# Agent attention and MLP in one kernel: block maxima added by TensorE to four score chunks, new load order and banks at the head

## The chip, the cores and the metric

The kernel runs on one core of a Trainium2 chip. The metric is device time in microseconds (us), the median of several executions; lower is better.

## The reference, cut to what matters

```python
def _attn_ref(q, k, v, agents):            # q, k, v: 2 x 12480 x 128; agents: 2 x 49 x 128
    scale = 1.0 / np.sqrt(q.shape[-1])
    def sm(a, b):
        s = scale * (a @ b.transpose(0, 2, 1))
        s = s - s.max(-1, keepdims=True)
        e = np.exp(s)
        return e / (e.sum(-1, keepdims=True) + 1e-09)
    agent_v = sm(agents, k) @ v            # 49 x 128 for each of the two batches
    return (sm(q, agents) @ agent_v).astype(np.float32)

def _moe_ref(x, w_in, w_out):              # x: 24960 x 128, d_ff = 2048
    h = x @ w_in
    return (np.maximum(0.01 * h, h) @ w_out).astype(np.float32)
```

The output is `_moe_ref(_attn_ref(q, k, v, agents).reshape(24960, 128), w_in, w_out)`. w_in and w_out come as 64-bit floats; the kernel makes 32-bit floats of their two halves itself.

## The kernel before, in words

Since `sm(q, agents)` is a matrix P of 49 columns, `x @ w_in` is `P @ (agent_v @ w_in)`: the kernel computes M = agent_v @ w_in once for each batch and then multiplies P by M. Products of full precision are made of two fp32r parts ("hi" and "lo"). The leaky relu is 0.99 relu plus 0.01 of the linear part, which is P @ (M @ w_out), with `ww` = 0.01 w_in @ w_out and l = agent_v @ ww.

**Main loop.** 52 blocks of 480 rows, eight steps in each. A step is `mm1` (six products with M, L785), `relu` (ACT makes hi, L798; DVE makes lo, L799) and, two steps later, `mm2` (twelve products with w_out, L815) into one of two PSUM pairs, `turns`. `mm1` has two PSUM pairs of its own. The attention of q for later blocks, the whole of batch 1 and other side work are hung into the steps by `at(step, function)`.

**Head.** Before block 0 the kernel does batch 0's agent attention over K and V in 13 chunks each (c = 0 to 12, 960 rows in a chunk), the conversion of w_in and w_out in eight pieces (w0 to w7, w_in and w_out in turn; w7 in the loop), P of blocks 0 and 1, and M. For a chunk of K, TensorE makes scores in one PSUM bank (`k_score`, L380), DVE takes them into a running maximum (`k_run`, L391), ACT copies them to SBUF (`k_copy`, L394). After the last chunk `k_max0` to `k_max3` (L405 to L429) find the maximum of each agent and spread it over the partitions, `k_sub` subtracts it from each chunk on DVE (L347), `k_exp` is the exponential on ACT (L438), and `k_av32` the product with V (L504). For a piece of w: `conv_bits` (masks, DVE, L263 and L264), `conv_mant` and `conv_exp` (ACT), `conv_low`, `conv_sign`, `conv_mul` (DVE, L279, L286, L293); w_out pieces then `wo_hi_of` and `wo_lo_of`. `ww_tr`, `ww_copy` and `ww_mm` (L310, L317, L323) transpose w_in and add up w_in @ w_out. At the end `f_copy` (L513), `f_den` (L523), `f_tr` (L531), `f_rec` (L537), `f_avT` (L543), then `m_half` and `m_mm` (L565, L575) make M, which `m_hi_of` and `m_lo_of` (L596, L600) scale and split. `p_two` copies P of block 0 out of that of block 1 by three DMAs (L763).

**Order.** `Plan` is a list scheduler that runs while the kernel is built: each step of the head has an engine, an assumed cost and the steps it follows; what can begin first comes next, with a per-kind `slack` added to its key. The instructions of an engine run in that order. Where TensorE's plan has a gap, `heat` products (L963) fill it. Loads are issued on SP in the order of `ORDER` (k, q, w, v), nine chunks of k and v in flight. `users` is the order in which steps take turns in the bank that `aux()` gives (q products, transposes, maximum, denominator).

Of the kernel before, what the change touches and what calls it, by code (L numbers as in the profile page):

```python
# [18 lines left out]
class Plan:  # L19
# [16 lines left out]
    def emit(self, idle):  # L36
# [16 lines left out]
        while len(done) < len(self.steps):  # L53
# [11 lines left out]
            if eng == idle[0] and begin > self.free.get(eng, 0) + idle[2]:  # L65
                idle[1](int((begin - self.free[eng] - 50) / idle[2]))
# [6 lines left out]
def tile_agent_attention_then_leaky_mlp(  # L73
# [51 lines left out]
    NP = NF // 2  # L125
    LD = 9
# [3 lines left out]
    ORDER = "kqwwkkwkkwkkkwkkkkkqwvvvvwvvvvvvvvvwq"  # L130
# [44 lines left out]
    ones = const.tile([P, P], F32, name="ones")  # L175
# [208 lines left out]

    def k_run(b, c):
        ps = sc_t[b, c][:TP, :CH * NA]
        r = run.rearrange("p j a -> p (j a)")
        if c == 0:
            nc.vector.tensor_copy(r, ps)
        else:  # L390
            nc.vector.tensor_tensor(out=r, in0=ps, in1=r, op=ALU.max)  # L391
# [11 lines left out]
    def k_max0(u):  # L403
        rm = p1.tile([TP, NA], F32, tag="rm", name="rm")
        nc.vector.tensor_reduce(  # L405
            out=rm, in_=run.rearrange("p j a -> p a j"), axis=AX.X, op=ALU.max
        )
        mb[u] = rm

    def k_max1(u):  # L410
        ps = aux()
        nc.tensor.transpose(ps[:NA, :TP], mb[u], ident[:TP, :TP])
        mb[u] = ps

    def k_max1d(u):
        m = p1.tile([NA, 1], F32, tag="m", name="m")
        nc.vector.tensor_reduce(out=m, in_=mb[u][:NA, :TP], axis=AX.X, op=ALU.max)
        dg = p1.tile([NA, NA], F32, tag="rm", name="dg")
        nc.vector.tensor_scalar(dg, ident[:NA, :NA], m, None, ALU.mult)
        mb[u] = dg  # L420

    def k_max2(u):
        ps = aux()
        nc.tensor.matmul(ps[:TP, :NA], lhsT=ones[:NA, :TP], rhs=mb[u], start=True, stop=True)
# [38 lines left out]
    NH = NCH * CH // G  # L463

# [27 lines left out]
    def av_zero(b, first):  # L492

        if first:
            av_t[b] = avw[0][:, :C + 2]
        z = pre[:TP, 0, :C + 2]
        nc.tensor.matmul(av_t[b], lhsT=z[:, :P], rhs=z, start=first, stop=not first)

    def k_av32(b, h):

        c, g = divmod(h, CH // G)
        for j in range(g * G, (g + 1) * G):
# [3 lines left out]
                start=False, stop=False,  # L506
# [13 lines left out]
    def f_den(b):  # L520
# [26 lines left out]
    mp_t, wp_t, mp_pair = {}, {}, []  # L547
# [331 lines left out]
    at(6, wo_lo_of, w7)  # L879
    at(7, k_m, 0, NM, 1)  # L880
# [60 lines left out]
    with tc.manual_schedule():  # L941
# [4 lines left out]
        nc.vector.memset(ones, 1.0)  # L946
# [4 lines left out]
        for o, a, n in SLOTS:  # L951
# [3 lines left out]
            )  # L955
        nc.gpsimd.memset(pd, 0.0)
# [3 lines left out]
        def heat(n, start=False):  # L960
# [16 lines left out]
            "k": (lambda c: load_k(0, c), 1210), "v": (lambda c: load_v(0, c), 1280),  # L977
            "w": (load_w, 1250), "q": (load_q, 610),
        }
        ring, held = [], {"k": ("run", "copy"), "w": ("low", "sign"), "v": ("vdone",)}  # L980
        sent, come = [], []
        for what, c in loads:
# [12 lines left out]
            cost += {2: 1700, 7: 1200}.get(len(come), 0)  # L995
            add((what, c), "dma", cost, lambda: None, (), [("trip", what, c)] + come[-1:], lag=0)
            come.append((what, c))
        for c in range(NCH):
            for g in range(2):
                after = [("k", c)] + [(x, c - 4) for x in ("run", "copy") if c >= 4]  # L1000
                after += [("s", c, 0)] * g
                add(("s", c, g), "pe", 560, k_score, (0, c, g, True), after, lag=150)
            after = [("s", c, 1)] + [("run", c - 1)] * (c > 0)
            add(("run", c), "dve", 485, k_run, (0, c), after)
            add(("copy", c), "act", 400, k_copy, (0, c), [("run", c)])
# [27 lines left out]
        add("two", "sp", 1350, p_two, (1,), [last, ("send", "v", NCH - 1)], lag=2000)  # L1033
        for m in range(NM):
            add(("tr", m), "pe", 620, ww_tr, (m,), [("mul", 2 * m)], lag=250)
            add(("wcopy", m), "act", 500, ww_copy, (m,), [("tr", m)])
            if m < NM - 1:
                add(("wmm", m), "pe", 1170, ww_mm, (m,), [("wcopy", m), ("mul", 2 * m + 1), "avopen"] + [("wmm", m - 1)] * (m > 0))
        last = ("run", NCH - 1)
        for fn, eng, cost in (  # L1040
            (k_max0, "dve", 780), (k_max1, "pe", 300), (k_max1d, "dve", 480),
# [103 lines left out]
```

## Time and profile before

| | us |
|---|---|
| median of 3 runs (lowest, highest) | 961.69 (960.86, 963.61) |
| the profiled execution, its time | 962.66 |
| the profiled execution, its span | 960.6 |
| TensorE busy (share of the span) | 946.2 (98%) |
| DVE busy | 737.7 (77%) |
| ACT busy | 612.4 (64%) |
| GpSimd busy | 374.0 (39%) |

The span runs from the first to the last instruction of that execution; its time also has what lies around the span. Busy shares are averages over the head and the loop, which have different limits. The rows of the trace name engines PE (TensorE), PEld (its weight loads), DVE, ACT, POOL (GpSimd) and SP (the queue that issues loads); times in them are us from the span's start, and L504 is line 504 of the kernel before. Every fp32 product is two records.

### The profile page before, as it was taken

How to read it: one execution, taken by the hardware profiler on the slowest of the kernel's cores; microseconds unless marked ns; L12 is line 12 of the kernel's file. 1: busy time of each engine (PE TensorE's matmuls, PEld its weight loads, DVE VectorE, ACT ScalarE, POOL GpSimd, SP SyncE). 2: the span in 40 equal slices, each digit the busy share in tenths (PEclk: the TensorE clock that was granted, in tenths of full speed). 3: DMA queues.
4: the chain of work that ended last, by engine and by line, in shares of the span. 5: the costliest groups of instructions: out<-in, count | busy, mean ns of one | idle time of the engine just before them, and what ended most of it. 6: DMA issues, size and time to landing. Idle time of an engine off the chain costs nothing.

```text
span 960.6 us, 22990 instructions
## 1 busy us (share of the span) xinstructions
PE 946.2 (98%) x9478; PEld 879.6 (92%) x9478; DVE 737.7 (77%) x1067; ACT 612.4 (64%) x908; POOL 374.0 (39%) x546
## 2 busy tenths in 40 slices
PE   8899999999999999999999999999999999999998
PEld 7767888888899899999988899999999999999897
DVE  7767677777888888888877777777777777777774
ACT  6655566566676666666666666666666666666654
POOL 0002243234566566565444434333343333343420
PEclk9999999999999999999999999999999999999999
DMA  9930322312312323222121111211111111112110
GB/s 341 404 115 24 122 74 83 114 32 64 94 53 71 86 63 86 62 63 73 34 57 37 43 52 32 63 33 52 42 43 53 43 53 42 53 42 53 32 42 21
DMA packets 29043, 70.74 MB, mean 74 GB/s; under 512 B 4467, under 2 KB 17907, under 8 KB 28939
## 3 DMA queue, kind: packets, MB, share of 16 engines
q1 hardware_dynamic: 28795, 69.16, 23.5%
q8 instruction: 74, 1.21, 0.5%
q14 instruction: 30, 0.25, 0.1%
q10 hardware_dynamic: 144, 0.12, 0.0%
HBM read 43.22 MB, written 12.78 MB: 58 GB/s over the span
## 4 chain that ended last, share of the span: by engine, by line
PE 95%; DMA 2%; DVE 1%; ACT 1%; issue 1%; SPq 0%; ACTq 0%
PE turn L815 57%; PE h L785 28%; PE turn L650 2%; PE turn L826 2%; PE turn L380 1%; PE turn L472 1%; PE turn L504 1%; DMA kt<-in_k_dram 1%; DMA w<-in_w_in_dram 1%; PE sc L380 1%; DVE lo L799 0%; PE turn L963 0%; PE turn L323 0%; ACT hi L798 0%; PE turn L575 0%
## 5 line engine op out<-in xcount | busy, mean ns | idle before, releaser
L799 DVE SCALAR_TENSOR_TENSOR lo<-h,hi 128x960 fp32r<-128x960 f32 x416 | 479.0, 1151 | 191.6 <-ACT hi L798 191.5
L798 ACT ACTIVATE hi<-h 128x960 fp32r<-128x960 f32 x416 | 405.9, 976 | 293.7 <-PE h L785 277.5
L815 PE MATMUL turn<-hi,wo_hi 64*128 64x480 f32 x1664 | 420.2, 380 | 0.0
L815 PE MATMUL turn<-hi,wo_lo 64*128 64x480 f32 x1664 | 416.9, 376 | 0.0
L785 PE MATMUL h<-pT,m_hi 64*128 64x480 f32 x1664 | 338.6, 377 | 0.5 <-DVE lo L799 0.4
L815 PE MATMUL turn<-lo,wo_hi 64*128 64x480 f32 x1664 | 337.7, 375 | 0.0
L815 PEld LDWEIGHTS turn<-hi,wo_lo 64*128 64x128 f32 x1664 | 261.2, 184 | 10.0
L815 PEld LDWEIGHTS turn<-hi,wo_hi 64*128 64x128 f32 x1664 | 257.4, 184 | 11.4 <-issue 1.5
L785 PEld LDWEIGHTS h<-pT,m_hi 64*128 64x128 f32 x1664 | 236.0, 184 | 12.6 <-DVE lo L799 0.8
L815 PEld LDWEIGHTS turn<-lo,wo_hi 64*128 64x128 f32 x1664 | 237.1, 184 | 11.1
L785 PE MATMUL h<-pT,m_lo 64*128 64x480 f32 x832 | 242.7, 375 | 0.0
L785 PEld LDWEIGHTS h<-pT,m_lo 64*128 64x128 f32 x832 | 139.0, 184 | 5.7
L347 POOL TENSOR_TENSOR qlo<-qt,qhi 128x480 fp32r<-128x480 f32 x50 | 61.2, 1225 | 78.8 <-DMA kt<-in_k_dram 63.4
L347 POOL TENSOR_TENSOR pT<-pt,pT 64x480 fp32r<-64x480 f32 x50 | 61.0, 1220 | 60.4 <-ACT pT L750 60.4
L693 POOL COPY mx<-mx 32x15 f32<-32x15 f32 x50 | 9.4, 188 | 184.8 <-DVE mx L686 178.3
L347 POOL TENSOR_TENSOR d<-st,mm 64x375 f32<-64x375 f32 x50 | 41.3, 826 | 94.6 <-DVE mm L699 94.6
L849 POOL TENSOR_TENSOR oT<-oT 128x480 f32<-128x480 f32 x51 | 62.5, 1225 | 12.8 <-issue 10.0
L838 ACT COPY oT<-turn 128x480 f32<-128x480 f32 x102 | 52.0, 562 | 1.1 <-PE turn L815 1.1
L736 POOL TENSOR_TENSOR pd<-d,rs 64x375 f32<-64x375 f32 x50 | 40.9, 817 | 28.9 <-DVE rs L731 28.9
L650 PE MATMUL turn<-qhi,a_hl 64*128 64x240 f32 x208 | 47.3, 275 | 1.2 <-DVE m_lo L600 0.7
L693 POOL COPY sm<-sm 32x15 f32<-32x15 f32 x50 | 9.4, 188 | 98.1 <-DVE sm L716 98.1
L650 PE MATMUL turn<-qlo,a_hl 64*128 64x240 f32 x208 | 47.1, 272 | 0.0
(146 smaller groups left out, 905.4 us busy)
## 6 DMA issues: line engine op xcount, KB each, us to landing
kt<-in_k_dram SPq DMA_DIRECT2D x26, 480.0 KB, 6.4
qt<-in_q_dram SPq DMA_DIRECT2D x52, 240.0 KB, 2.9
pT<-pT SPq DMA_DIRECT2D x104, 120.0 KB, 2.3
out_dram<-oT SPq DMA_DIRECT2D x51, 240.0 KB, 2.0
vt<-in_v_dram SPq DMA_DIRECT2D x13, 520.0 KB, 9.5
vt<-in_v_dram SPq DMA_DIRECT2D x13, 487.5 KB, 4.5
w<-in_w_in_dram SPq DMA_DIRECT2D x4, 512.0 KB, 9.3
w<-in_w_out_dram SPq DMA_DIRECT2D x4, 512.0 KB, 8.9
```

What stands on the lines that cost most here:

```text
L347: eng.tensor_tensor(out=o, in0=x, in1=y, op=ALU.subtract)
L380: nc.tensor.matmul(ps[r, j * NA:(j + 1) * NA], lhsT=k_t[b, c][:, j, r], rhs=a_sb[:, b, :], start=True, stop=True,)
L650: nc.tensor.matmul(s_t[i][:, m, :h], lhsT=a_hl[i // BPB][r], rhs=x[r, m * h:(m + 1) * h], start=(s == 0 and n == 0), stop=(n == 1), skip_g ...
L693: by(i).tensor_copy(r[x, :, 1], r[y, :, 0])
L736: by(i).tensor_tensor(out=pd[:n, :, :A0], in0=d[:n], in1=w[:n].to_broadcast([n, NT, A0]), op=ALU.mult,)
L785: nc.tensor.matmul(ps[:, g, :NB], lhsT=w[b][r, cols(2 * p + g)], rhs=t[r, x], start=(n == 0), stop=(n == 2),)
L798: nc.scalar.activation(hi, ps, AF.Relu)
L799: nc.vector.scalar_tensor_tensor(out=lo, in0=ps, scalar=0.0, in1=hi.bitcast(F32), op0=ALU.max, op1=ALU.subtract,)
L815: nc.tensor.matmul(o[g][:, :NB], lhsT=w[r], rhs=x[r], start=start, stop=stop)
L826: nc.tensor.matmul(o[g][:, :NB], lhsT=w[b][r], rhs=t[r, x], start=False, stop=False)
L838: nc.scalar.copy(t[:, g], o[g][:, :NB])
L849: nc.gpsimd.tensor_tensor(out=t[:, 0], in0=t[:, 0], in1=t[:, 1], op=ALU.add)
```

## The change

Scores of chunks 9 to 12 of batch 0 stay in PSUM, in rows of 50 instead of 49 columns. After the maximum, `k_top` lets TensorE add minus the maximum to them, as one fp32r product of a matrix of ones with a matrix that has the maxima on its diagonal in two parts (`top`); `k_exp` reads them from PSUM. They have no `k_copy` and no `k_sub`. The products with V begin with these four chunks (`TURN`), and v is loaded in that order. Chunks 0 to 3 get their scores from products of full width (120 columns of weights), not two halves. `ORDER` is new. The closing zero product of the accumulation goes. The transpose and the two halves of M get PSUM banks of their own, and the transpose comes ahead of the denominator. Piece 1 of M, the third w_out product and `ww_part` move from the head into step 1 of the loop, the rest of M and of w7 to later steps. Heat is put in with 300 ns less in each gap, and none ahead of the last steps of the head. Costs and slacks of the plan are new.

```diff
-            if eng == idle[0] and begin > self.free.get(eng, 0) + idle[2]:
-                idle[1](int((begin - self.free[eng] - 50) / idle[2]))
+            gap = begin - self.free.get(eng, 0) - idle[3]
+            if eng == idle[0] and gap > idle[2] and name not in idle[4]:
+                idle[1](int(gap / idle[2]))
...
+    NS = 4
+    NW = 4
...
-    ORDER = "kqwwkkwkkwkkkwkkkkkqwvvvvwvvvvvvvvvwq"
+    ORDER = "qwkkwkwkkwkkqkkkkkkvvvvvwvvvvwwvvvvwq"
...
         ps = sc_t[b, c]
+        w = NA + late(b, c)
+        whole = b == 0 and c < NW
         for j in range(g * CH // parts, (g + 1) * CH // parts):
-            for r in (slice(0, HALF), slice(HALF, TP)):
+            for r in (slice(0, TP),) if whole else (slice(0, HALF), slice(HALF, TP)):
                 nc.tensor.matmul(
-                    ps[r, j * NA:(j + 1) * NA], lhsT=k_t[b, c][:, j, r], rhs=a_sb[:, b, :],
-                    start=True, stop=True,
+                    ps[r, j * w:j * w + NA], lhsT=k_t[b, c][:, j, r], rhs=a_sb[:, b, :],
+                    start=j == 0 or not late(b, c), stop=True,
+                    skip_group_check=late(b, c),
                 )
+    def late(b, c):
+        return b == 0 and c >= NCH - NS
...
     def k_max0(u):
...
+        for o in (0, HALF):
+            nc.vector.tensor_reduce(
+                out=wide[:, o:o + NA], in_=run.rearrange("p j a -> p a j"), axis=AX.X,
+                op=ALU.max,
+            ) if o == 0 else nc.vector.tensor_copy(wide[:, o:o + NA], wide[:, :NA])
...
     def k_max1d(u):
...
+        nc.vector.tensor_reduce(out=m, in_=mb[u][:EW, :TP], axis=AX.X, op=ALU.max)
+        nc.vector.tensor_scalar(top, less, m, None, ALU.mult)
+        r = slice(HALF, EW)
+        nc.vector.scalar_tensor_tensor(
+            out=top[r], in0=less[r], scalar=m[r], in1=top[r].bitcast(F32),
+            op0=ALU.mult, op1=ALU.subtract,
+        )
...
+    def k_top(b, c):
+
+        ps = sc_t[b, c][:TP, :CH * (NA + 1)].rearrange("p (j a) -> p j a", j=CH)
+        t = top[:, None, :].to_broadcast([EW, CH, NA + 1])
+        nc.tensor.matmul(ps, lhsT=ones, rhs=t, start=False, stop=True, skip_group_check=True)
...
+    TURN = [(n - NS) % NCH for n in range(NCH)]
...
     def f_tr(b):
         t = av_t[b]
+        if b == 0:
+            tr_t[b] = single("tr")
...
-        if h == 0:
-            mp_pair.append(single("mp"))
         c = slice(h * MC // 2, (h + 1) * MC // 2)
-        ps = mp_t[b, h / 2] = mp_pair[-1][:, c]
+        ps = mp_t[b, h / 2] = single("mp")[:, :MC // 2]
...
-    at(0, k_m, 0, 2)
-    at(0, conv_bits, w7)
-    at(1, conv_exp, w7, 0)
-    at(2, k_m, 0, 3)
+    at(1, k_m2, 0, 1)
+    at(1, ww_mm, NM - 2)
+    at(1, ww_part)
+    at(1, conv_bits, w7)
+    at(2, conv_exp, w7, 0)
     at(3, conv_exp, w7, 1)
     at(4, conv_mant, w7, nc.scalar)
     at(4, conv_sign, w7)
+    at(5, k_m, 0, 3)
     at(5, conv_low, w7)
-    at(5, conv_mul, w7, nc.vector)
-    at(6, ww_mm, NM - 1)
-    at(6, ww_end)
+    at(6, conv_mul, w7, nc.vector)
     at(6, wo_hi_of, w7, nc.scalar)
-    at(6, wo_lo_of, w7)
-    at(7, k_m, 0, NM, 1)
+    at(7, ww_mm, NM - 1)
+    at(7, ww_end)
+    at(7, wo_lo_of, w7)
+    at(8, k_m, 0, NM, 1)
...
-        add("two", "sp", 1350, p_two, (1,), [last, ("send", "v", NCH - 1)], lag=2000)
+        add("two", "sp", 1800, p_two, (1,), [last, ("send", "v", NCH - 1)], lag=2300)
...
-            (f_copy, "act", 230, "avend"), (f_den, "pe", 150, f_copy),
-            (f_tr, "pe", 250, f_den), (f_rec, "dve", 330, f_den), (f_avT, "act", 230, f_tr),
+            (f_copy, "act", 270, ("av", NH - 1)), (f_tr, "pe", 400, f_copy),
+            (f_den, "pe", 200, f_tr), (f_avT, "act", 270, f_tr), (f_rec, "dve", 330, f_den),
...
-        for n, fn, args in ((0, m_half, (0, 0)), (0.5, m_half, (0, 1)), (1, m_mm, (0, 1))):
+        for n in (0, 0.5):
...
+        add("go", "pe", 1300, lambda: None, (), [("mhi", 0), "two"])
...
-            (("tr", 1), ("wcopy", 1)), (k_max1, k_max1d), (k_max2, k_max3),
-            (("chain", 1, 2), ("chain", 1, 5)), (("tr", 2), ("wcopy", 2)),
-            (("tr", 3), ("wcopy", 3)), (f_den, f_avT),
+            (("tr", 1), ("wcopy", 1)), (("chain", 1, 2), ("chain", 1, 5)),
+            (k_max1, k_max1d), (k_max2, k_max3), (("tr", 2), ("wcopy", 2)),
+            (("tr", 3), ("wcopy", 3)), (f_den, f_rec),
...
-            plan.emit(("pe", heat, 270))
+            plan.emit(("pe", heat, 270, 300, (f_tr, f_den, ("mm", 0), ("mm", 0.5), "go")))
...
-        owner[0] = 0
-        ww_part()
```

## Rows read from the trace of the kernel before

**Rows 1.** Table of stages: us, engines' busy time (count), granted clock, DMA share, GB/s.
```profile
31.97:36.40 4.43, 4.43 (x41) 4.14 (x41) 2.73 (x7) 0.49 (x1) 0.00 (x0) 0.63 1.02 409
53.40:59.00 5.60, 4.79 (x29) 3.66 (x27) 2.85 (x8) 2.59 (x7) 0.00 (x0) 1.00 0.41 88
59.00:81.00 22.00, 19.12 (x144) 14.08 (x146) 15.82 (x22) 12.96 (x19) 1.58 (x3) 1.00 0.26 79
81.00:103.00 22.00, 22.00 (x251) 19.40 (x251) 15.14 (x23) 13.19 (x20) 7.51 (x13) 1.00 0.25 80
```

**Rows 2.** Chain of waits, head: start, length, engine, tile and line.
```profile
30.05 1.91 issue
31.97 0.84 PE sc L380 x21
...
38.63 4.59 PE turn L504 x80
...
53.43 0.43 PE turn L497 x2
...
54.26 0.49 PE turn L963 x2
...
56.88 0.86 PE turn L575 x2
...
58.92 1.04 PE h L785 x6
```

**Rows 3.** Timeline, block 0: start, length, engine, line, operation, [idle <-releaser].
```profile
64.15 0.49 PE L815 MATMUL turn<-hi,wo_hi 64*128 64x480 f32 x2
...
67.52 0.39 PE L650 MATMUL turn<-qlo,a_hl 64*128 64x240 f32 x2
...
75.76 1.13 PE L323 MATMUL turn<-w_out_sb,pre 128*128 128x128 f32 x8 [1.74 <-DVE w_out_sb L293]
...
80.83 0.60 PE L785 MATMUL h<-pT,m_hi 64*128 64x480 f32 x4
```

**Rows 4.** Timeline of SP: the issue of V's last chunk.
```profile
42.37 0.33 SPq L212 DMA_DIRECT2D vt<-in_v_dram  x1
```

**Rows 5.** DMA issues in 42.2 to 42.75: count, size, us to landing.
```profile
vt<-in_v_dram SPq DMA_DIRECT2D x1, 520.0 KB, 7.0
```

**Rows 6.** Timeline after the last score.
```profile
33.46 0.83 DVE L405 TENSOR_REDUCE rm<-run 120x49 f32<-120x392 f32 x1
...
35.15 0.41 PE L412 MATMUL turn<-ident,rm 120*49 120x120 f32 x1
...
35.90 0.24 DVE L419 TENSOR_SCALAR dg<-ident,m 49x49 f32<-49x49 f32 x1
```

**Rows 7.** Timeline of the tail: ACT and SP.
```profile
54.15 1.82 SPq L763 DMA_DIRECT2D pT<-pT  x3
...
55.43 0.27 ACT L543 COPY avT<-turn 128x128 f32<-128x128 f32 x1 [1.22 <-DVE den L537]
...
56.91 0.84 ACT L596 ACTIVATE m_hi<-mp,rec 128x256 fp32r<-128x256 f32 x2 [1.22 <-PE mp L565]
...
58.27 0.50 SPq L767 DMA_DIRECT2D pT<-pT  x1
```

**Rows 8.** Timeline of DVE: masks (L263) and last products (L293) of w chunks.
```profile
7.86 0.43 DVE L263 TENSOR_SCALAR em<-w 128x512 int32<-128x512 int32 x1 [0.41 <-DMA w<-in_w_in_dram]
...
12.65 0.68 DVE L293 TENSOR_TENSOR w_in_sb<-w_in_sb,e 128x512 f32<-128x512 f32 x1
...
36.06 0.41 DVE L263 TENSOR_SCALAR em<-w 128x512 int32<-128x512 int32 x1
...
40.45 0.43 DVE L263 TENSOR_SCALAR em<-w 128x512 int32<-128x512 int32 x1
...
48.87 0.69 DVE L293 TENSOR_TENSOR w_in_sb<-w_in_sb,e 128x512 f32<-128x512 f32 x1
...
55.51 0.67 DVE L293 TENSOR_TENSOR w_out_sb<-w_out_sb,e 128x512 f32<-128x512 f32 x1
```

More of the change, by code (lines that the diff above doesn't have):

```diff
@@ L174, in tile_agent_attention_then_leaky_mlp @@
     turn = const.tile([P, 2, 1], F32, name="turn")
-    ones = const.tile([P, P], F32, name="ones")
+    ones = const.tile([HALF + NA, TP], F32R, name="ones")
+    less = const.tile([HALF + NA, NA + 1], F32, name="less")
+    top = const.tile([HALF + NA, NA + 1], F32R, name="top")
+    wide = const.tile([TP, P], F32, name="wide")
     sel = const.tile([EW, P], F32, name="sel")
@@ L403, in k_max0 @@
     def k_max0(u):
[L404 to L408, printed above, removed]
+        for o in (0, HALF):
[3 more added lines that the diff above has]
+            ) if o == 0 else nc.vector.tensor_copy(wide[:, o:o + NA], wide[:, :NA])
     def k_max1(u):
         ps = aux()
-        nc.tensor.transpose(ps[:NA, :TP], mb[u], ident[:TP, :TP])
+        nc.tensor.transpose(ps[:EW, :TP], wide[:, :EW], ident[:TP, :TP])
         mb[u] = ps
     def k_max1d(u):
[L416 to L420, printed above, removed]
+        m = p1.tile([EW, 1], F32, tag="m", name="m")
+        nc.vector.tensor_reduce(out=m, in_=mb[u][:EW, :TP], axis=AX.X, op=ALU.max)
[5 more added lines that the diff above has]
+        )
     def k_max2(u):
         ps = aux()
-        nc.tensor.matmul(ps[:TP, :NA], lhsT=ones[:NA, :TP], rhs=mb[u], start=True, stop=True)
+        nc.tensor.matmul(ps[:TP, :NA + 1], lhsT=ones, rhs=top, start=True, stop=True)
         mb[u] = ps
@@ L490, in e_zero, with av_zero @@
         nc.gpsimd.memset(er[r].bitcast(F32), 0.0)
-    def av_zero(b, first):
-        if first:
-            av_t[b] = avw[0][:, :C + 2]
+    def av_zero(b):
+        av_t[b] = avw[0][:, :C + 2]
         z = pre[:TP, 0, :C + 2]
-        nc.tensor.matmul(av_t[b], lhsT=z[:, :P], rhs=z, start=first, stop=not first)
+        nc.tensor.matmul(av_t[b], lhsT=z[:, :P], rhs=z, start=True, stop=False)
     def k_av32(b, h):
-        c, g = divmod(h, CH // G)
+        n, g = divmod(h, CH // G)
+        c = TURN[n]
         for j in range(g * G, (g + 1) * G):
@@ L505, in k_av32 @@
                 av_t[b][o:o + NA], lhsT=s_sb[:, c, j, :], rhs=v_t[b, c][:TP, j, :],
-                start=False, stop=False,
+                start=False, stop=h == NH - 1 and j >= CH - 2,
             )
@@ L955, in tile_agent_attention_then_leaky_mlp @@
             )
+        nc.gpsimd.tensor_tensor(
+            out=less, in0=ident[:EW, :NA + 1], in1=ident[:EW, HALF:EW + 1], op=ALU.add
+        )
+        nc.gpsimd.tensor_scalar(less, less, -1.0, None, ALU.mult)
         nc.gpsimd.memset(pd, 0.0)
@@ L976, in tile_agent_attention_then_leaky_mlp @@
         fetch = {
-            "k": (lambda c: load_k(0, c), 1210), "v": (lambda c: load_v(0, c), 1280),
+            "k": (lambda c: load_k(0, c), 1210),
+            "v": (lambda n: load_v(0, TURN[n]), 1280),
             "w": (load_w, 1250), "q": (load_q, 610),
         }
-        ring, held = [], {"k": ("run", "copy"), "w": ("low", "sign"), "v": ("vdone",)}
+        ring, held = [], {"k": ("run",), "w": ("low", "sign"), "v": ("vdone",)}
         sent, come = [], []
@@ L994, in tile_agent_attention_then_leaky_mlp @@
             add(("trip", what, c), (what, c), 1500, lambda: None, (), sent)
-            cost += {2: 1700, 7: 1200}.get(len(come), 0)
+            cost += {2: 900, 6: 600, 8: 800, 15: 900}.get(len(come), 0)
             add((what, c), "dma", cost, lambda: None, (), [("trip", what, c)] + come[-1:], lag=0)
@@ L1001, in tile_agent_attention_then_leaky_mlp @@
                 after += [("s", c, 0)] * g
-                add(("s", c, g), "pe", 560, k_score, (0, c, g, True), after, lag=150)
+                add(("s", c, g), "pe", 560 if c >= NW else 860, k_score, (0, c, g, True), after, lag=150)
             after = [("s", c, 1)] + [("run", c - 1)] * (c > 0)
             add(("run", c), "dve", 485, k_run, (0, c), after)
-            add(("copy", c), "act", 400, k_copy, (0, c), [("run", c)])
+            if not late(0, c):
+                add(("copy", c), "act", 400, k_copy, (0, c), [("run", c)])
         for n in range(w7):
@@ L1077, in tile_agent_attention_then_leaky_mlp @@
         slack = {
[L1078 to L1080 removed]
+            "tr": 400, "wmm": 800, "wohi": 2000, "wolo": 1200, "bits": 400, "mant": 300,
+            "exp": 100, "low": 400, "sign": 800, "mul": 600, "sub": 600, "copy": 1200,
+            "run": 200, "wcopy": 200, "av": 200,
         }
```

62 lines of the change are left out of this document (34 added, 28 removed).

## The prediction

> **What bounds the kernel now.** I read the table of stages first. From 81 us on TensorE is busy without a gap (22.00 of 22.00), so every microsecond by which that state comes earlier is one of the total, and so is TensorE work that is taken out of what is left then; the diff takes none. Before it, in 59 to 81, TensorE is idle for 2.9 us, where block 0 starts up [rows 1]. So there are two questions: when does the first product of block 0 (L785) start, now 58.92, and how long is it from there to block 1's first, now 80.83, which is 21.9 us later [rows 2, 3].
>
> Second, the chain of waits. Before 58.92 it is TensorE from 38.6 on: the products with V (L504) run from 38.63 to 53.43 with little between them but transposes and heat, 0.92 us for a chunk of 16 records (4.59 for five). Then comes a serial tail: closing product, copy, heat, denominator, transpose, copy, two halves of M, a third piece of M, products of w_out [rows 2]. Third, the loads: the last chunk of V is issued at 42.37 and lands 7.0 us later, at 49.4 [rows 4, 5]. So V is not what holds the head: TensorE ends 4.0 us after it because it began late. It began late because the last score was ready only at 32.81, after 1.91 us in which TensorE stood in the middle of a chunk with nothing named, and because from there to the first product it took 5.8 us [rows 2].
>
> **The change, part by part.**
>
> *Maximum on TensorE, four chunks first.* Now, after the last score: running maximum, reduction ending at 34.29, transpose at 35.15 behind four heats at a granted clock near 0.5, diagonal done at 36.14, then broadcast, copy, subtraction, exponential, and at 38.57 the first product [rows 1, 2, 6]. The new chain has one more copy of 49 columns and one more small DVE product (0.24 each, by the diagonal's row), and loses the copy to SBUF (0.21) and the subtraction (about 0.5) on the way to the first product. The 400-column fp32r product is not in the trace; the nearest rows are 0.39 for 240-column and 0.60 for 480-column pieces, two to four of them together [rows 3], I take 0.3 and nothing hangs on it. New: maximum 0.6, reduction 0.85, copy 0.25, transpose 0.45, three DVE steps with hops 1.05, product 0.3, exponential 0.5, hops 0.2: 4.2 us, where it was 5.8. DVE loses four subtractions, ACT four copies.
>
> *Loads.* Ahead of the last k chunk there is one w chunk less and one q chunk more: 272 KB less, 0.67 us at the 409 GB/s of the stage [rows 1]. Whether TensorE is then ready is open: the stall may stay (last score 32.8) or go (about 30). Ahead of the last v chunk the bytes are the same and the DMA share is 1.0 already, so it lands at 49.4 again. Four score chunks at full width cost TensorE more time and half the instructions; heats run in that place now, and they cover it (without them about 0.6 us a chunk). The constants made on POOL and DVE at the start are hidden behind the first loads.
>
> *End of the products with V.* Started 4.2 us after a last score at 30 to 32.8, they begin at 34.2 to 37.0. Thirteen chunks at 0.92 to 1.02 and two transposes at 0.65 make 13.3 to 14.6 us, so TensorE could be through at 47.5 to 51.6, and the last chunk can't end before 49.4 + 1.1 = 50.5. With three planned heats of 0.42 the late case is 52.9. I take 51.1, nearer the load's row, because TensorE has slack against it in all but the late case. Before: 53.43.
>
> *The tail.* Gone: the closing product 0.43, the heat ahead of the denominator 0.49, the denominator ahead of the transpose, the wait of avT's copy for DVE's read (the copy began at 55.43, released by that read), half of M's pair (each half has a bank now, so the scaling starts after the first), the third piece of M 0.86, w_out's products 0.89 and their closing one 0.24; the last three go into the loop. Left: hop 0.08, copy 0.28, hop 0.04, transpose 0.47, copy with hops 0.34, half of M 0.56, hop 0.04, scaling 0.42 (0.84 for two), hop 0.07: 2.3 us, where it was 5.5 [rows 2, 7]. The denominator runs beside this: product 0.2, two small DVE steps 0.4, done some 1.5 us after the end, the scaling needs it at 1.8. The three pT copies on SP come at 54.15 now, because DVE does the q chain among the subtractions [rows 7, 8]; with q's load seven places earlier that chain fits into DVE's idle pieces before 36, the copies go out behind the last v and are there before 53. If it doesn't, they hold L785 as now (issued from 54.15 to 55.97, landed by 58.27, when SP's next copy starts).
>
> The 0.2 us and the half above come from banks: ACT's copy waited for DVE's read of another column of the same tile [rows 7]. The Trainium skill (PSUM — Partial Sum Buffer, PSUM bank collisions) keeps two engines apart by bank, whatever their columns, and the trace agrees. By that rule the moved steps pay as well where they share banks with the q chain, which speaks against the change; the waits in block 0 below are worked out without it.
>
> So L785 starts at 51.1 + 2.3 = 53.4 (52.8 to 55.2): 5.5 us earlier (6.1 to 3.7).
>
> *Block 0.* What left the tail stands in step 1: pieces 1 and 2 of M as a pair, w_out's third product and its closing, 2.0 us more on TensorE, 0.7 on ACT, 0.75 on DVE. Counted from L785's start, with the durations of the same operations in the rows: first relu done at 2.1, its DVE partner at 3.3, second relu 3.1, the two scalings 3.8 and 4.5, their DVE partners 5.1 and 5.8. The first L815 must wait for the last of these, because they read the pair of banks that it writes: 5.8, now 5.2 [rows 3]. Then w7's mask, its exponent, q_hi and, on POOL, q_lo (1.2) stand ahead of the q products, done at 9.4, now 9.0. From there five second products at 1.31, four first at 0.66, 0.2 of q, 0.86 of M, 0.9 of w_out: 11.2. Two waits: M's last piece needs q's sum to be read out of the same tile (DVE at 14.8, TensorE there at 13.6: 1.2), and the w_out product needs w7's last DVE step (0.8; now 1.7). Block 1 begins at 22.7, now 21.9, and the product for l (0.4) is still to come: 1.2 us given back. Bounds: 2.0 given back, if all moved work adds and no wait goes; 0.9 gained, if it fills idle time and w7's wait goes.
>
> Sum: 5.5 - 1.2 = 4.3 us. The profiled execution took 962.66 (span 960.6), so 958.4 for one like it; it lies 0.97 above the median shown. From the median, rounded: 961.7 - 4.2 = **957.5**. About 0.3%, 2.9 us, is what this measurement can tell from no change: under 958.8 is faster, over 964.6 slower.
>
> **Rivals.**
>
> *w6 comes too late (0.14).* w5 and w6 now follow v8. With four v chunks behind it (2.08 MB at 400 GB/s, 5.2 us) w6 lands at 44.2. The order of the banks puts the denominator behind w6's transpose and copy. The first w conversion ran from 7.86 to 13.33, 5.5 us; w6's took 9.1, 40.45 to 49.56 [rows 8]. With 5.5 it ends at 49.7, transpose and copy at 51.0, in time; up to 6.7 us do no harm. With 9.1: 53.3, copied at 54.6, reciprocal 55.2, L785 at 55.7, gain 3.2 - 1.2 = 2.0: 959.7. For it: DVE still has subtractions and w5 to do then. Against: four subtractions (about 0.5 each) and the q chain (about 7 us, an estimate from its 20 steps) leave DVE there, w4's conversion enters (2.9: masks 0.42 twice, then three steps at 0.69) [rows 8].
>
> *The products with V don't end earlier (0.06).* If exponentials or V's sends pace them, only the tail is gained, 3.1 - 1.2 = 1.9: 959.8. Against: now TensorE hardly waits for either [rows 2].
>
> *Clock (0.06).* After the 1.91 us stall the granted clock averaged 0.63 over 4.43 us, most of it at TensorE's 1.2 GHz [rows 1]. The tail and step 0 get no heat now. One such fall costs half of about 3.6 us, 1.8: 959.3. Against: idle pieces of 0.4 us in the tail left it at 1.00 [rows 1, 2]. The Trainium skill (TensorE: Matmul & The Clock Gate, Part 1) has an idle array throttled to 1.2 GHz, which speaks against taking heats out; the trace agrees after the stall and not in the tail.
>
> *Slower: w5 blocks the start of block 0 (0.08).* The third w_out product needs w5's conversion, and all of the head's DVE work is queued ahead of the first relu's partner. w5's mask now begins at 36.06 and its last product ends at 56.18, 20.1 us later [rows 8]. Left to the end again from its landing at 42.9, it ends at 63.0, its rest at 63.7, and the partner starts there instead of at 53.4 + 2.1 = 55.5: 8.2 us, 965.7. It eats the gain from an end at 59.0 on and is slower by 0.3% from 61.9 on. Against: DVE has then no more to do than now.
>
> **Numbers.** The forecast has 0.62 (its own range 955.2 to 958.8), and 0.04 go to a larger gain. The rivals near 959.7 are held, the slower one left out: 955.2 to 961.2. Faster is the forecast and the larger gain, 0.66; same the three rivals between, 0.26; slower 0.08.
>
> **What would show it.** The last score before 32.8; L504 first on chunk 9, at 34 to 37, and last at 50.5 to 52; from there 2.3 to 2.6 to L785, at 53 to 54; 22 to 23.5 from it to block 1; clock 1.00 from 50 on. Wrong if the reciprocal releases the scaling (w6), if L504 ends after 52.5, if the pT copies end last, if DVE does w5 after 55, or if block 0 takes over 25.

## The result, and the profile after

The changed kernel takes 969.73 us (median of 4 runs, 969.00 to 971.42) against 961.77 of the kernel before beside it: 1.0083 of its time, 95% interval 1.0063 to 1.0103. It is slower by 8.0 us, where 4.2 us faster was forecast, and the time lies above the whole range. The profiled execution took 969.59, its span is 967.8 (960.6 before).

Where the 7.2 us of span come from: the first product of block 0 starts at 62.95 (before 58.92: 4.0 later, forecast 5.5 earlier); from there to block 1 it takes 24.2 us (before 21.9: 2.3 more, forecast 0.8 more); what is left behind it takes 880.6 (before 879.8: 0.9 more with rounding, forecast 0.4 for l).

The table of stages of the kernel after, columns as in [rows 1]: us, busy time (count) of PE, PEld, DVE, ACT and POOL, granted clock, DMA share, GB/s.

```profile
6.50:8.50 2.00, 0.00 (x0) 0.00 (x0) 0.46 (x3) 1.49 (x4) 0.00 (x0) 1.00 1.01 389
...
9.80:15.00 5.20, 5.20 (x28) 5.20 (x28) 1.84 (x4) 0.62 (x1) 0.00 (x0) 0.50 1.02 388
15.00:20.50 5.50, 5.50 (x29) 5.50 (x29) 2.71 (x6) 1.94 (x5) 0.00 (x0) 0.50 1.02 414
20.60:25.70 5.10, 5.10 (x50) 4.92 (x49) 2.61 (x5) 3.48 (x7) 0.00 (x0) 0.50 0.94 350
...
28.50:29.30 0.80, 0.80 (x21) 0.80 (x19) 0.00 (x0) 0.80 (x3) 0.00 (x0) 0.50 0.68 276
29.30:30.60 1.30, 1.30 (x38) 1.25 (x35) 0.93 (x2) 0.24 (x1) 0.00 (x0) 0.84 0.00 0
30.60:32.00 1.40, 1.40 (x34) 1.23 (x35) 1.40 (x4) 0.58 (x1) 0.00 (x0) 1.00 0.96 217
...
62.95:87.17 24.22, 20.21 (x152) 14.95 (x154) 15.79 (x20) 13.24 (x19) 1.57 (x3) 1.00 0.18 56
```

Read the clock column beside the busy column. TensorE does nothing in 6.50 to 8.50; from 9.80 on it is busy for all of the time, at 0.50, that is 1.2 GHz, until past 28.50. A share of 100% hides it: in 5.20 us it gets through 28 records. The DMA share falls to 0 at 29.30: the chunks of K are not used up, their buffers are not free, and the loads behind them, V's among them, wait. From 20 to 50 SP stands for 10.2 us, in eight waits, behind score products (L388) with the loads of V.

TensorE's timeline of the kernel after, columns as in [rows 3]:

```profile
8.56 0.38 PE L679 MATMUL turn<-qhi,a_hl 64*128 64x240 f32 x2 [2.11 <-ACT turn L671]
...
9.79 9.69 PE L388 MATMUL sc<-a_sb,kt 128*120 128x49 f32 x48
...
20.58 5.16 PE L388 MATMUL sc<-a_sb,kt 128*120 128x49 f32 x48
...
27.67 2.98 PE L388 MATMUL sc<-a_sb,kt 128*64 128x49 f32 x64
...
43.56 9.74 PE L532 MATMUL turn<-vt,s_sb 120*49 120x130 f32 x144
53.23 1.60 PE L999 MATMUL turn<-pre 128*128 128x128 f32 x12
...
62.95 0.77 PE L814 MATMUL h<-pT,m_hi 64*128 64x480 f32 x4 [1.08 <-DVE m_lo L629]
...
69.58 0.48 PE L844 MATMUL turn<-hi,wo_hi 64*128 64x480 f32 x2 [1.02 <-DVE m_lo L629]
...
72.77 0.38 PE L679 MATMUL turn<-qlo,a_hl 64*128 64x240 f32 x2 [0.86 <-POOL qlo L353]
...
78.53 1.13 PE L604 MATMUL turn<-w_in_sb,avT 128*128 128x512 f32 x2 [1.23 <-DVE sq L703]
...
84.68 1.16 PE L329 MATMUL turn<-w_out_sb,pre 128*128 128x128 f32 x8 [0.90 <-DVE w_out_sb L299]
...
87.17 0.60 PE L814 MATMUL h<-pT,m_hi 64*128 64x480 f32 x4
```

The idle time ends with ACT's `turn` copy: two elements, which order the two halves of the q products. ACT's timeline of the kernel after shows what it stood behind (the copy is L671):

```profile
6.98 1.48 ACT L279 ACTIVATE e<-e,off 128x512 int32<-128x512 int32 x2 [2.43 <-DVE e L270]
8.36 0.14 ACT L671 COPY turn<-turn 128x2 f32<-128x2 f32 x1
```

The first half of the q products was done by 6.45, and the copy could have run then; but the exponents of a w chunk (L279) come first in ACT's order and waited for DVE. The Trainium skill (PSUM — Partial Sum Buffer, Engine vs sequencer instructions) has ACT's queue strictly in order, and the trace agrees. In the kernel before the same copy cost TensorE 0.25 us, by TensorE's timeline there:

```profile
7.90 0.39 PE L650 MATMUL turn<-qhi,a_hl 64*128 64x240 f32 x2 [0.25 <-ACT turn L642]
```

The plan does not have the copy as a step of ACT's, so nothing in it saw the wait.

Full-width scores are 16 records a chunk. Half tiles, which use 64 and then 56 columns of weights instead of 120, are 32. Three full-width chunks in 9.69 us are 3.2 each; the next row is one full-width and one half-tile chunk, which leaves 1.9 for the half tiles; the clock comes back during the two half-tile chunks from 27.67 on. The last score ends at 38.27 (before 32.81), the first product with V starts at 43.56 (before 38.57), and twelve records of heat at 53.23 stand where V is not there yet.

### The profile page after: what moved, and what is told of

It is laid out like the page before. It is cut to its first block, busy times and chain, and to the rows that moved or that the text cites. A ratio compares the mean times of both kernels' runs of the same rounds, so it can differ in the third digit from the quotient of the medians.

```text
span 967.8 us, 22788 instructions
## 1 busy us (share of the span) xinstructions
PE 952.2 (98%) x9380; PEld 882.3 (91%) x9380; DVE 737.2 (76%) x1068; ACT 609.9 (63%) x904; POOL 374.5 (39%) x548
## 4 chain that ended last, share of the span: by engine, by line
PE 96%; DVE 2%; ACT 1%; DMA 0%; issue 0%; POOL 0%; SPq 0%; ACTq 0%; DVEq 0%
PE turn L844 57%; PE h L814 28%; PE turn L679 2%; PE sc L388 2%; PE turn L855 2%; PE turn L532 1%; PE turn L388 1%; PE turn L500 1%; DMA w<-in_w_in_dram 0%; PE turn L604 0%; PE turn L329 0%; PE turn L999 0%; DVE run L408 0%; PE turn L316 0%; DVE m_lo L629 0%
## 5 line engine op out<-in xcount | busy, mean ns | idle before, releaser
L844 PE MATMUL turn<-hi,wo_hi 64*128 64x480 f32 x1664 | 422.8, 380 | 1.0 <-DVE m_lo L629 1.0
L844 PE MATMUL turn<-hi,wo_lo 64*128 64x480 f32 x1664 | 419.5, 376 | 0.0
L814 PE MATMUL h<-pT,m_hi 64*128 64x480 f32 x1664 | 343.2, 377 | 1.1 <-DVE m_lo L629 1.1
L844 PE MATMUL turn<-lo,wo_hi 64*128 64x480 f32 x1664 | 342.5, 375 | 0.0
L844 PEld LDWEIGHTS turn<-hi,wo_lo 64*128 64x128 f32 x1664 | 258.3, 184 | 10.8
L844 PEld LDWEIGHTS turn<-hi,wo_hi 64*128 64x128 f32 x1664 | 254.3, 184 | 13.2 <-issue 1.5
L844 PEld LDWEIGHTS turn<-lo,wo_hi 64*128 64x128 f32 x1664 | 236.9, 184 | 12.2
L814 PEld LDWEIGHTS h<-pT,m_hi 64*128 64x128 f32 x1664 | 235.8, 184 | 13.2 <-DVE m_lo L629 1.5
L814 PE MATMUL h<-pT,m_lo 64*128 64x480 f32 x832 | 243.8, 376 | 0.0
L814 PEld LDWEIGHTS h<-pT,m_lo 64*128 64x128 f32 x832 | 137.4, 184 | 6.8 <-DVE m_lo L629 0.2
```

Of the source, the lines that this page charges most:

```text
L814: nc.tensor.matmul(ps[:, g, :NB], lhsT=w[b][r, cols(2 * p + g)], rhs=t[r, x], start=(n == 0), stop=(n == 2),)
L844: nc.tensor.matmul(o[g][:, :NB], lhsT=w[r], rhs=x[r], start=start, stop=stop)
```

## The experiments

Each ratio is to the kernel before, run beside it on the same chip (medians 962.14 to 962.35), with its 95% interval. L814 is the first product of block 0 and L844 the second kind, `mm2` (L785 and L815 in the kernel before). In the kernels with two added lines they are L816 and L846. "Fill" is this edit, nine heat products between the halves of block 0's q products:

```diff
     def q_mm(i):
         s_t[i] = ps = aux2()
         q_half(i, 0)
+        if i == 0:
+            heat(9)
         nc.scalar.copy(turn, ps[:, :, :1])
```

**e1_halves, e2_gap_filled, e3_before_wide, e4_halves_filled: idle time or full width.** e1 is the changed kernel with `NW = 0`, e2 with the fill, e4 with both. e3 is the kernel before with nothing but full width for the first four chunks:

```diff
-            for r in (slice(0, HALF), slice(HALF, TP)):
+            for r in (slice(0, TP),) if b == 0 and c < 4 else (slice(0, HALF), slice(HALF, TP)):
...
-                add(("s", c, g), "pe", 560, k_score, (0, c, g, True), after, lag=150)
+                add(("s", c, g), "pe", 560 if c >= 4 else 860, k_score, (0, c, g, True), after, lag=150)
```

> Changed kernel with the scores of chunks 0 to 3 in two halves again (plan costs with them), all else as changed. Theory A (the full-width scores, 3.2 us a chunk at a granted clock of 0.50 from 9.8 to 27.7 us, cost the time; the rest of the change does roughly what the prediction said): the clock comes back before 15 us, the last score is ready before 33, block 0 starts at 53 to 55, time 956 to 959.5. Theory B (the new load order and plan are late by themselves): 965 to 969.

> Changed kernel, full-width scores kept, nine heat products put between the two parts of block 0's q products, where TensorE stood idle for 2.11 us just before the clock fell. If that idle piece is what loses the clock (A1): clock 1.00 through the full-width scores, at about 1.6 us a chunk, block 0 at 54 to 56, time 957 to 961. If full-width scores lose the clock by themselves (A2): it falls to 0.50 some us after they begin although TensorE has not been idle, time 966 to 970.

> Kernel before with only the scores of chunks 0 to 3 at full width. There TensorE has no long idle piece ahead of them and heat between them. A1: clock stays up, the scores cost 0.5 us a chunk that heat had, time 960 to 963. A2: clock falls to 0.50 among them, last score 3 us or more later, time 963 to 968.

> Changed kernel with halves and with the nine heat products in the gap. Both theories of the clock: as with halves alone, at most 1 us faster, since the clock never falls there: 955.5 to 959. Theory B: 965 to 969 here too.

Time and ratio are of all executions of a kernel; the five columns behind them are of the one that was profiled.

| | us | ratio (95%) | last score | V products | first L814 | block 0 | span |
|---|---|---|---|---|---|---|---|
| after | 969.73 | 1.0083 (1.0063, 1.0103) | 38.27 | 43.56 to 59.25 | 62.95 | 24.2 | 967.8 |
| e1 | 962.64 | 1.0003 (0.9994, 1.0012) | 32.26 | 36.45 to 52.13 | 55.83 | 25.8 | 962.3 |
| e2 | 962.66 | 1.0005 (0.9995, 1.0015) | 31.05 | 35.26 to 51.52 | 55.21 | 25.8 | 961.7 |
| e4 | 962.80 | 1.0006 (0.9995, 1.0017) | 31.65 | 36.20 to 51.42 | 55.13 | 25.8 | 961.7 |
| e3 | 960.60 | 0.9981 (0.9966, 0.9996) | 30.70 | 35.43 to 51.00 | 56.49 | 21.9 | 958.0 |

The table of stages of e1, with the idle time and half tiles:

```profile
8.50:10.00 1.50, 1.46 (x7) 1.25 (x8) 1.26 (x2) 1.07 (x2) 0.00 (x0) 0.50 1.02 415
...
11.00:12.00 1.00, 1.00 (x27) 1.00 (x26) 0.00 (x0) 0.00 (x0) 0.00 (x0) 0.55 1.09 420
12.00:13.00 1.00, 1.00 (x38) 1.00 (x34) 0.75 (x2) 0.15 (x1) 0.00 (x0) 1.00 0.95 351
```

The same for e2, without the idle time and with full width:

```profile
9.00:15.00 6.00, 6.00 (x58) 6.00 (x59) 4.44 (x10) 2.97 (x5) 0.00 (x0) 1.00 1.02 400
```

And e2's timeline: three full-width chunks at 1.00, and the end of the head.

```profile
9.42 5.14 PE L388 MATMUL sc<-a_sb,kt 128*120 128x49 f32 x48
...
50.42 1.10 PE L532 MATMUL turn<-vt,s_sb 120*49 120x130 f32 x16 [1.05 <-DMA vt<-in_v_dram]
51.44 0.66 PE L316 MATMUL turn<-ident,w_in_sb 128*128 128x128 f32 x4
52.02 0.46 PE L562 MATMUL tr<-sel,avs 113*128 113x128 f32 x2
52.77 0.38 PE L551 MATMUL turn<-avs,sel 113*128 113x1 f32 x2 [0.30 <-ACT pre L323]
53.02 1.11 PE L594 MATMUL mp<-w_in_sb,avT 128*128 128x256 f32 x4
55.21 0.96 PE L816 MATMUL h<-pT,m_hi 64*128 64x480 f32 x4 [1.08 <-DVE m_lo L629]
```

Neither is enough alone here. With the idle time and half tiles the clock falls to 0.50 and is back within 12 to 13; with full width and the gap filled it does not fall; with the idle time and full width it stays down for 20 us. Each undoing brings the time down by 7 us, and both together by no more: one loss with two conditions. The fill puts heat where the idle time was, so no run tells the lack of idle time from the heat a little ahead of the scores. At 1.00 a full-width chunk takes 1.71 us (5.14 for three). In the kernel before full width alone is worth 0.2%: in e3's trace the last score is 2.1 us earlier, and the unnamed stalls in the scores, 0.80 and 1.91 us before, come to 0.34.

But with the clock back the change is worth nothing yet: L814 starts 3.7 us earlier than before in e2, and block 0 takes 3.9 longer. So e1, e2 and e4 all lie above the times that I had expected of them.

**e11_turn_on_dve and e12_wide_gap: the wait itself, and the pair without the change.** e11 is the changed kernel with the copy taken out of ACT's queue; e12 is e3 without the nine heat products that ran at 9.35 to 11.36.

```diff
-        nc.scalar.copy(turn, ps[:, :, :1])
+        (nc.vector.tensor_copy if i == 0 else nc.scalar.copy)(turn, ps[:, :, :1])
```

```diff
         def heat(n, start=False):
+            n = 0 if n > 4 and not start else n
```

> The changed kernel, and nothing else moved but the two-element copy between the two halves of the q products of block 0: DVE makes it instead of ACT, where it stood behind 1.48 us of exponent conversion. The masks on DVE end at 6.95, so the copy ends at about 7.1 and TensorE is idle for some 0.7 us instead of 2.11, with nothing put into the idle time. Theory (the idle 2.11 us took the clock down, and full-width scores did not bring it back): granted clock 0.95 to 1.00 from 8 to 25, about 1 us for a full-width chunk at the end of them, last score at 30 to 32, first product of block 0 at 55 to 56.5, block 0 25.5 to 26 with its clock fall in the tail, time 962 to 963.5, ratio to before 1.000 to 1.002. Rival (full-width scores take the clock down by themselves in this order): 0.50 from 10 on, 969 to 970. Between them: 0.7 us idle is also enough for a fall, and the time is 969 again though the idle time is a third.

> The kernel before with full-width scores of the first four chunks (it was faster than before by 0.2%), but without the nine heat products that stood between the q products and the second chunk, at 9.35 to 11.36. That leaves TensorE idle for about 2 us and then gives it full-width scores, with nothing else of the change in it. Theory: granted clock near 0.50 from 11.5 until half-tile scores come, 3.2 us for each of the three remaining full-width chunks, so that the half tiles begin at about 22 instead of 19.6, last score 33 to 36 (30.7 with the heat), and a time of 962 to 966. Rival (the idle time alone is not enough, or a clock at 0.50 comes back within a few us of full-width scores as it does with half tiles): last score under 32, time 960 to 961.5.

e11: 967.74 us (its runs spread from 962.39 to 970.00), ratio 1.0050 (1.0027, 1.0073). e12: 963.33, ratio 1.0013 (1.0004, 1.0023), which is 0.3% more than e3. The table of stages of e11's profiled execution (965.11 us):

```profile
9.80:11.50 1.70, 1.70 (x18) 1.68 (x17) 1.63 (x5) 0.26 (x1) 0.00 (x0) 1.00 1.03 423
11.50:13.00 1.50, 1.50 (x14) 1.47 (x12) 1.50 (x4) 1.47 (x3) 0.00 (x0) 0.84 1.01 372
13.00:14.00 1.00, 1.00 (x7) 1.00 (x7) 0.44 (x1) 0.72 (x2) 0.00 (x0) 0.50 1.01 404
...
21.30:22.30 1.00, 1.00 (x6) 0.78 (x4) 0.96 (x4) 0.60 (x1) 0.00 (x0) 0.50 1.02 415
22.30:23.30 1.00, 1.00 (x30) 0.99 (x30) 0.69 (x1) 0.97 (x3) 0.00 (x0) 0.77 1.02 411
23.30:24.30 1.00, 1.00 (x42) 1.00 (x38) 0.61 (x2) 0.88 (x2) 0.00 (x0) 1.00 1.00 407
```

And of e12:

```profile
9.40:10.70 1.30, 0.04 (x1) 0.00 (x1) 1.05 (x3) 1.27 (x4) 0.00 (x0) 0.79 1.04 417
10.70:11.70 1.00, 1.00 (x5) 1.00 (x6) 0.86 (x2) 0.97 (x2) 0.00 (x0) 0.50 1.02 346
...
13.00:25.64 12.64, 12.64 (x85) 12.23 (x84) 8.27 (x17) 7.08 (x14) 0.00 (x0) 0.50 1.02 411
...
26.60:28.00 1.40, 1.40 (x45) 1.40 (x42) 0.47 (x1) 0.00 (x0) 0.00 (x0) 0.78 1.05 416
```

e12 shows the pair with nothing else of the change: 1.3 us idle, then full width, and the clock is 0.50 until half tiles have run from 25.64 on; the last score is at 35.29 instead of 30.70. e11 misses my number. The idle time is down to 0.80 us, and in the profiled execution the clock still fell, only later, at about 12.5, after more than 4 us of full-width scores at 1.00 without a gap. So a shorter wait is not a cure, and here the fall comes in full-width work itself. It came back in both during a run of half tiles (from 22.31 in e11).

The mean granted clocks of the other executions say how far this carries. The four of the kernel after have 0.985 to 0.989, and those of e1, e2 and e4 0.995 to 1.000: there time and clock go together. In e11 the three longest executions (969.68 to 970.00) have 0.996, above the 0.990 of the profiled one, so a longer stay at 0.50 is not what makes them the longest; what does was not profiled. In e12 eight of ten have 0.991 to 0.993, and the two with 0.997 and 0.999 are not shorter (966.48 and 963.40). So e12 shows the fall by its trace, and not by its time.

**e5_tail_heat and e6_m_order: why block 0 gives it back.** e5 is e4 with two heat products behind `f_tr` and four behind the second half of M. e6 is e4 with the pieces of M one by one:

```diff
-    at(1, k_m2, 0, 1)
+    at(0, k_m, 0, 1)
+    at(1, k_m, 0, 2, 1)
...
+    at(2, k_m, 0, 3)
...
-    at(5, k_m, 0, 3)
```

> Halves and filled gap (962.8 us, block 0 starts at 55.13, granted clock 0.66 in 55 to 60), with two heat products after the head's transpose and four after the halves of M. Theory C (the head's 3.8 us are lost partly to the clock, which falls in the tail without heat): clock 1.00 in 55 to 60, the twelve records of the first two steps take 1.65 us, not 2.43, M's pair 1.9, not 2.7, time 961.0 to 961.6. Theory D alone (the order of M in block 0 holds everything, whatever the clock): within 0.4 of 962.8.

> Halves and filled gap, with M's pieces single again: piece 1 in step 0, piece 2 in step 1, piece 3 in step 2 (before the q products), not a pair in step 1 and piece 3 in step 5. Theory D: the first L815-like product no longer waits for two scalings and two DVE steps in a row, and the wait of piece 3 for the q sum (1.2 us) goes: block 1's first product 1.5 to 3 us earlier, time 960.0 to 961.3. Theory C alone: within 0.5 of 962.8, the clock still falls.

e5: 962.32, 0.9997 (0.9988, 1.0006), block 0 24.2 instead of 25.8. e6: 961.66, 0.9995 (0.9986, 1.0004), block 0 23.4. The table of stages of e4:

```profile
55.00:60.00 5.00, 4.87 (x16) 2.98 (x17) 3.08 (x4) 2.01 (x3) 0.00 (x0) 0.66 0.58 161
```

And of e5:

```profile
55.00:60.00 5.00, 4.81 (x30) 3.21 (x28) 3.53 (x5) 2.84 (x4) 0.00 (x0) 1.00 0.65 171
```

1.6 us of block 0 in e4's profiled execution is the clock, which falls after a tail in which TensorE was idle for 1.4 of 3.7 us. In e5, with heat there, it is 1.00, and what stays, 24.2, is what the kernel after has at 1.00 throughout. The idle time in the tail does not decide it alone: the kernel after has the same tail (busy for 2.3 of 3.7 us) and e6 no heat in it, and both were granted 1.00 there. Since e5 and e6 both have 1.00 in 55 to 60, the order of the pieces is worth the 0.8 us between 24.2 and 23.4.

Not every execution seems to have this fall. Four of e4's ten, the profiled one among them, have a mean clock of 0.996 and took 963.44 to 965.71; the other six have 0.999 or 1.000 and took 962.34 to 963.03. That fits the ratios, in which both gains are 0.1%, no more than the intervals. Both times lie between what I had given to the two theories, so the times decide nothing here and the traces carry it.

**e7_all: the mends together.** The changed kernel with full width, fill, the tail heat, single pieces and the denominator ahead of the fourth transpose (`(f_den, f_rec)` before `(("tr", 3), ("wcopy", 3))` in `users`).

> Changed kernel with full-width scores, filled gap, tail heat, single pieces of M, and the denominator ahead of the fourth transpose in the bank's order. If C and D add up and the order of the bank costs what the trace shows (about 1 us between the last product with V and block 0): 957.5 to 959.5, faster than both kernels. If they hide each other: 960 to 962.

961.47, ratio 0.9999 (0.9986, 1.0011). It misses: block 0 took 23.4, but the last chunk of V was there 1.3 us later than in e2, and L814 started at 56.61. What delayed V was not found. One of its twelve executions took 967.75 at a mean clock of 0.988, as low as in the kernel after, although the gap is filled; it was not profiled, so the fill may not hold the clock every time.

**e8_no_top: what the sums on TensorE are worth.** e4 with `NS = 0`: no chunk gets its maximum on TensorE.

> Halves and filled gap, with no late chunks: the maximum is subtracted by DVE in all 13 chunks, V in its own order. If V's last chunk (landed at about 50.2) sets the end of the products with V, as in the run with halves and filled gap, the maximum on TensorE is worth nothing there: within 0.5 of 962.8. If the first product's start sets it: it starts some 1.6 us later and the time is 964 to 965.

967.00 (964.75 to 968.55), ratio 1.0052 (1.0034, 1.0069). The median misses by far. The profiled execution is the shortest of the four, 964.75, so its trace accounts for less than half of the 4.2 us that the median is above e4; what the others lost is in no trace. ACT's timeline of e8:

```profile
55.07 0.58 ACT L323 COPY pre<-turn 128x512 f32<-128x512 f32 x1 [1.13 <-PE turn L316]
56.52 0.84 ACT L625 ACTIVATE m_hi<-mp,rec 128x256 fp32r<-128x256 f32 x2 [0.87 <-DVE rec L570]
```

The products with V end at 51.83, 0.4 later than in e4, but the first product of block 0 starts at 58.01, 2.9 later. With four subtractions more, DVE is at its w products until 53.1, the fourth transpose and its copy come late, the denominator stands behind that copy in the order of the bank, and the scaling of M waits for the reciprocal. This is my first rival (the copy ahead of the denominator too late), in the variant without the DVE time that the change frees.

**e9_block0_back and e10_before_wide_tail: the parts that pay.** e9 is e2 with block 0 as before: piece 1 of M, the third w_out product and `ww_part` ahead of the loop, the steps of w7 and M where they were. e10 goes from the other side: e3 with the new tail, and no other part of the change:

```diff
-                start=False, stop=False,
+                start=False, stop=h == NH - 1 and j >= CH - 2,
...
+        if b == 0:
+            tr_t[b] = single("tr")
...
-        ps = mp_t[b, h / 2] = mp_pair[-1][:, c]
+        ps = mp_t[b, h / 2] = single("mp")[:, :MC // 2]
...
-        add("avend", "pe", 350, av_zero, (0, False), [("av", NH - 1)])
...
-            (f_copy, "act", 230, "avend"), (f_den, "pe", 150, f_copy),
-            (f_tr, "pe", 250, f_den), (f_rec, "dve", 330, f_den), (f_avT, "act", 230, f_tr),
+            (f_copy, "act", 270, ("av", NH - 1)), (f_tr, "pe", 400, f_copy),
+            (f_den, "pe", 200, f_tr), (f_avT, "act", 270, f_tr), (f_rec, "dve", 330, f_den),
```

> Changed kernel with full-width scores and filled gap (962.66 us, block 0 starts at 55.21, takes 25.8 us), and with the whole of block 0 as before: piece 1 of M, the third w_out product and its closing again ahead of step 0, the rest of M and of w7 in their old steps. Theory D (work moved into block 0 costs more there than its absence saves in the tail, since block 0 goes by one wait after the other): block 0 starts 1 us later, about 56.2, since TensorE has 1.08 us of waiting to fill there, but takes 21.9 us again and leaves 0.9 us less behind it; the clock stays up; 958.5 to 960.0, faster than before by 0.2 to 0.35%. Rival (the moved work is free in block 0 and its cost was the clock's): 961 to 963.

> Kernel before with the full-width scores and the new tail alone (transpose ahead of the denominator, banks of their own for it and the halves of M, no closing product); load order, maximum, heat and block 0 as before. With the full-width scores alone it took 960.6, block 0 starting at 56.49, 5.5 us after the last product with V. If the tail's edits save what the prediction had for them apart from the moved work (about 1.2 us): start at 55.2 to 55.6, time 958.8 to 960. If the wait for both DVE halves of M holds the start, as in the changed kernel: no earlier than 56.2, time 960 to 961.

e9: 960.17, ratio 0.9980 (0.9971, 0.9989), just above my range; L814 at 56.17 as expected, block 0 23.3 in the profiled execution, which took 1.1 more than the median and had the clock at 0.52 in 74.3 to 77.4. Half of those 3.1 us, about 1.5, is what that costs, an estimate from these two numbers, and without it block 0 would take about the 21.9 of the kernel before. e10: 958.94, ratio 0.9971 (0.9961, 0.9982), the fastest here, ahead of both kernels. The timeline of e10's tail:

```profile
50.90 0.71 PE L964 MATMUL turn<-pre 128*128 128x128 f32 x4 [0.42 <-ACT avs L513]
51.45 0.39 PE L534 MATMUL tr<-sel,avs 113*128 113x128 f32 x2
51.67 0.28 PE L523 MATMUL turn<-avs,sel 113*128 113x1 f32 x2
51.81 0.47 PE L964 MATMUL turn<-pre 128*128 128x128 f32 x2
52.19 1.13 PE L566 MATMUL mp<-w_in_sb,avT 128*128 128x256 f32 x4
53.16 1.02 PE L576 MATMUL turn<-w_in_sb,avT 128*128 128x512 f32 x2
54.02 1.05 PE L323 MATMUL turn<-w_out_sb,pre 128*128 128x128 f32 x8
54.91 0.39 PE L330 MATMUL turn<-pre 128*128 128x128 f32 x2
55.22 0.71 PE L786 MATMUL h<-pT,m_hi 64*128 64x480 f32 x4
```

The work that the change moves into block 0 stands here in the tail, where it covers the scaling of M and keeps TensorE busy at 1.00; block 0 then takes 21.7. The first product at 55.22 is as early as in e2, with nothing to give back.

e9 has the new load order and the maximum on TensorE, e10 has neither and is 1.2 us faster. So no run here shows the part that gives the change its name to pay beside the order of the kernel before; e8 shows only that the changed order is slower without it.

## Why the prediction was wrong

**The step that failed** is the one on loads: "Four score chunks at full width cost TensorE more time and half the instructions; heats run in that place now, and they cover it (without them about 0.6 us a chunk)." The 0.6 was right at the full clock: 1.71 against 1.10 for a half-tile chunk (e10) is 0.6. At 0.50 it is 3.2 against 1.9, and the clock did not come back in it: the last score is 5.5 us later than before, where I had it as early or earlier. I had a rival "clock", but put it into the tail and priced it at 1.8, and I never asked what stood ahead of the full-width chunks in the new order: that ACT's small copy would come behind a w chunk's exponents. That follows from `ORDER`, which loads q and w first now: before, the copy ran at 7.69 and the first exponents (L273) only from 9.43. e1, e2 and e12 show the two conditions, e11 that a shorter wait does not do.

**The head without that.** In e2: last score 31.05 (forecast 30 to 32.8), first product with V 4.2 us later (4.2), and the products with V ended at 51.5 (51.1) with the landing of V's last chunk as the bound. These steps held, but for the landing: TensorE waited for that chunk until 50.42, and I had it there at 49.4. The tail is 3.7 us instead of 2.3: the fourth transpose of w_in (0.66) runs first, the denominator waits for its copy by the order of the bank and M's halves stand behind the denominator, and the first product is released by the split of both halves, where I had counted the scaling. So 3.7 us of gain, not 5.5.

**Block 0.** Forecast 22.7, measured 24.2 at clock 1.00. The waits for q's sum (1.23 against 1.2) and for w7 (0.90 against 0.8) came as worked out. The first L844 started 6.6 after the first L814 instead of 5.8, because the two pieces of M in one tile, though each has a bank of its own in it, let ACT's second scaling start only when DVE had read the first (ACT's timeline of the kernel after, below). So the wait in [rows 7], which I put down to the bank, may be one of the tile as well. The q products waited another 0.86 for POOL. The clock rival then came true at its place, 1.6 against the 1.8 forecast, in the profiled executions of e1, e2 and e4; the row it rests on, 4.43 us at 0.63, makes 3.3 us at 0.50 and not 3.6, and so 1.6.

```profile
68.05 0.69 ACT L625 ACTIVATE m_hi<-turn,rec 128x512 fp32r<-128x512 f32 x1 [0.82 <-DVE m_lo L629]
```

And what is left behind block 0 is 0.9 to 1.1 longer in the changed kernels, not the 0.4 of l, and 0.3 longer in e9, so most of it comes with the work that was moved; where it lies was not looked for. That adds to -3.7 + 3.9 + 0.9 = 1.1 for e2, and the span of its profiled execution is 1.1 longer. Its median is 0.05% above the kernel before, inside the interval.

**The other rivals.** "w6 too late" did not happen in the change and did in e8. "V products don't end earlier" and "w5 blocks the start" did not happen in e2. In the kernel after the products with V did end later, at 59.25, but for the late scores and not for the reason that the rival has.

## What to carry to other kernels

Before an edit that makes one stage cost more at the full clock, look for the idle time ahead of it in the new order, small unplanned copies in another engine's queue included, and price the stage at 0.50 as well. A stage that is 100% busy may be at half clock: read count and clock, not the share. Work taken out of a tail is a gain only if nothing there was covered by it: putting it back made e9 2.5 us shorter than e2. Look at the clock of every execution too, not only of the one that was profiled.

## What was not expected of the hardware

With the clock at 0.50, TensorE went through full-width fp32 scores, transposes and w_out products for 15 us in e12 and 18 in the kernel after with no gap, and stayed there; a run of half tiles (half the width, twice the count) saw it rise 0.5 to 2.1 us after its start in e1, e11, e12 and the kernel after, by the mean clock of the slices around the rise, while a single half-tile chunk between full width and other work had not. In e11 it fell in the midst of such full-width work, in e2 and e3, with nine heat products a little ahead, the same work held 1.00. What decides it was not found out.

The unnamed stalls in the scores, [rows 2] has the one of 1.91 us, have a fixed place: counted in pairs of product and weight load from TensorE's first, they stand after the 346th or 347th or the 473rd pair in the six kernels where I counted (e1 1.32 us and e4 1.78 after the 473rd, e2 1.50 and e3 0.34 after the 346th). 126 pairs are 252 instructions. The Trainium skill (Runtime: NRT & Kernel Launch, Instruction fetch mechanics) has instructions fetched in blocks of 256, mostly hidden; the spacing agrees, and if that is what they are, hidden they are not while the DMA share is 1.0. The traces bear on it. They have a DMA queue named instruction (q8), whose packets are 16 KB. In all eleven unnamed stalls that I find in the scores, 0.18 to 2.13 us long, such a packet moves 2.3 to 2.7 us before the stall ends. Where there is no such stall (the kernel after, e7, e9, e11), TensorE comes to the 346th pair 2.5 us or more after the packet. So TensorE goes on a fixed time after that packet, however long it stood; no run moved a packet to test it.
